# mLSTM with routed experts on one core: k of a pair's heads in one transfer, scores in 64x64 quadrants, the last columns of x and the logits half a step later

## The chip, the cores and the metric

The kernel runs on one core of one Trainium2 chip. The metric is the device time of one execution in microseconds (us). Most executions of a kernel agree within 0.3%.

## What is computed

The reference is an mLSTM layer (a linear attention with gates) followed by a mixture of experts of which each token uses one.

```python
# q, k, v, o_gate: (4, 8, 768, 40) = batch, heads, tokens, dims; i_gate, f_gate: (4, 8, 768)
for t in range(768):
    m_new = maximum(f_gate[t] + m, i_gate[t])
    f, i = exp(f_gate[t] + m - m_new), exp(i_gate[t] - m_new);  m = m_new
    C = f * C + i * outer(v[t], k[t])            # 40 x 40 for each batch and head
    n = f * n + i * k[t]
    y[t] = sigmoid(o_gate[t]) * (C @ q[t]) / maximum(abs(n @ q[t]), 1)
x = y as (4 * 768, 8 * 40)
logits = normalized(x) @ normalized(expert_emb).T / tau      # 8 experts
e = argmax(logits);  out = softmax(logits)[e] * relu(x @ w1[e]) @ w2[e]
```

All inputs are float32. The weights are 320x1024 and 1024x320 for each expert.

## The kernel before

**Tiling.** The recurrence is not run token by token. A window is 128 tokens of one batch entry, and one *half step* n (0 to 23) handles all eight heads of one window: `j, b = divmod(n, 4)` names the window j and the batch entry b. Two half steps, 2q and 2q + 1, share one set of loaded inputs, number q. Within a half step the window is cut into two chunks c of L = 64 tokens. Products inside a chunk are computed directly (a 64x64 matrix of *scores* for each head and chunk, masked by `late` and applied to the gated values `uv`); what comes from earlier tokens goes through a state, `c_st` from one window to the next and `c_mid` from the first chunk to the second.

**How k and q lie.** Heads are held two and two: dims 0 to 39 of one head in partitions 0 to 39, those of the other in partitions 64 to 103. `q_s` holds both, with zeros in the other 48 partitions, and comes in one transfer of 128 partitions. k is held in two tiles: `k_e` has only the upper heads (partitions 0 to 39), `k_o` only the lower ones (64 to 103), and the rest of both is set to zero once per buffer, by memsets and by a multiplication with zero on ScalarE (`zero_act`). `stage_k` issues one transfer of 40 partitions for each. `stage_scores` (line 629) multiplies all 128 rows of `k_e` or `k_o` with all 128 of `q_s`, so that the zeros leave one head. One such product has 64 columns of output partitions (r * 64 onward) and 64 moving columns, and all 16 of a half step go to one bank of PSUM, `s`. `stage_weigh` (line 645) multiplies the bank by the mask on VectorE.

**One half step on TensorE**, in the order of the code: `stage_add(n, 0)` (state and first chunk into the bank `y`, lines 664 and 674), `stage_scores(n + 1)` (line 637), `stage_y(n)` (line 712: weighted scores times `uv`; line 725: q times the two states), `stage_add(n, 1)` (second chunk into the state, line 674). In n = 4 and in the odd n from 5 on, between lines 712 and 725, `stage_xts` transposes what two half steps left of x: 128 tokens, in five pieces of 64 columns for each of two half steps, four pieces to the bank `px` and the fifth to the bank `pj` (line 792). At the end of the same half step `stage_logits` (line 812) multiplies the transposed `xt` by the expert embeddings into the bank `pm`.

**The other engines.** ScalarE copies the state's middle (`c_mid`, line 690), gathers x for the transpose (`xc`, line 785), takes the sum of squares (`junk`, line 771), copies `px` and `pj` to `xt` (lines 798 and 799), takes the sigmoid of the output gate (line 736) and casts pieces of the first expert's weights (line 197). VectorE weighs, normalizes (`den`, `x`) and carries the routing along: `route` appends routing operations to a list, and `tick` takes the next ones off it at fixed places. GpSimd computes `uv`, the output gate's product and parts of the weights. SyncE (SP) issues nearly all transfers.

**What sets the order.** The kernel schedules by hand: each engine runs its instructions strictly in the order in which the code emits them, and waits are placed only where data or a buffer require them. PSUM has eight banks: `pX` one, `pM` two, `pY` three, `pS` one, `pJ` one.

**After the half steps** the last tokens are routed, and the experts run as matrix products of 128 to 512 tokens (lines 390 and 428).

Of the kernel before, what the change touches and what calls it, by code (L numbers as in the profile page):

```python
# [26 lines left out]
P = 128  # L27
# [39 lines left out]
def tile_mlstm_moe(  # L67
# [470 lines left out]
    with ExitStack() as actx:  # L538
# [7 lines left out]
        pS = ictx.enter_context(tc.tile_pool(name="pS", bufs=1, space=PSUM, side="right"))  # L546
        pJ = ictx.enter_context(tc.tile_pool(name="pJ", bufs=1, space=PSUM, side="right"))
# [25 lines left out]
        k_e, k_o, q_s, kv_s, kr_s, vr_s, uv, w_s = [], [], [], [], [], [], [], []  # L573
        for i in range(NB):
            k_e.append(ap1.tile([P, 2, NP, P], F32, name=f"k_e{i}"))
            k_o.append(ap1.tile([P, 2, NP, P], F32, name=f"k_o{i}"))
# [5 lines left out]
            w_s.append(ap1.tile([P, 2, NP, L], F32, name=f"w_s{i}"))  # L582
# [46 lines left out]
        def stage_scores(n):  # L629
            q, k = divmod(n, 2)  # L630
            s = st.setdefault(n, {})["s"] = pS.tile([P, 2, NP, L], F32, name=f"s_{n}", tag="ps")
            for c in range(2):
                cs = slice(c * L, c * L + L)
                for a in range(NP):
                    for r in range(2):
                        m = a // 2 * 2 + r
                        T.matmul(  # L637
                            s[r * L : r * L + L, c, a],
                            (k_e, k_o)[a % 2][q % NB][:, k, m, cs],
                            q_s[q % NB][:, k, m, cs],  # L640
                            start=True,
                            stop=True,
                        )

        def stage_weigh(n):
            V.tensor_tensor(  # L646
                w_s[n % NB].rearrange("p c a t -> p (c a) t"),
                st[n]["s"].rearrange("p c a t -> p (c a) t"),
                late.unsqueeze(1).broadcast_to([P, 2 * NP, L]),
# [55 lines left out]
        def stage_y(n, mid=None):  # L705
# [4 lines left out]
            for a in range(NP):  # L710
                for c in range(2):
                    T.matmul(  # L712
                        y[c * L : c * L + L, a * 2 * D1 : (a + 1) * 2 * D1],
                        w_s[n % NB][:, c, a],
# [72 lines left out]
        def stage_xts(q, pool, tag):  # L787
            xc = xc_.pop(q)
            px = pX.tile([P, 512], F32, name=f"px_{q}", tag="px")
            pj = pool.tile([P, 512], F32, name=f"pj_{q}", tag=tag)  # L790
            for c in range(NX):
                T.transpose(  # L792
                    px[:, c * P : (c + 1) * P] if c < 4 else pj[:, 0:P],
                    xc[:, c].rearrange("p i f -> p (i f)"),
                    ident,
                )
            xt = st[2 * q]["xt"] = tp.tile([P, NX, P], F32, name=f"xt_{q}", tag="xt", bufs=1)
            A.copy(xt[:, 0:4], px.rearrange("p (c t) -> p c t", c=4))
            A.copy(xt[:, 4], pj[:, 0:P])
# [220 lines left out]
        def early_ids():  # L1020
# [18 lines left out]
            5: ([], [(route_a, 0, 0, SAMPLE), (sample,)]),  # L1039
# [7 lines left out]
            15: ([lambda: route_ids(0)], [(route_d, 0), (route_a, 1)]),  # L1047
# [4 lines left out]
        }  # L1052
        vq = []
# [11 lines left out]
        def route(n, i):  # L1065
            if i == 0:
# [15 lines left out]
        def flat(t):  # L1082
            return t.rearrange("p n a t -> p (n a t)")

        def zero_act(t):

            A.activation(
                flat(t).rearrange("p (g t) -> p g t", t=P),
                onef.unsqueeze(1).broadcast_to([P, 2 * NP, P]),
                AF.Copy,  # L1090
                scale=0.0,
            )

        fill(FILLS[0])
        V.memset(k_e[0][:, 0], 0.0)
        G.memset(k_o[0][:, 0], 0.0)
# [6 lines left out]
        V.memset(k_e[0][:, 1], 0.0)  # L1103
# [5 lines left out]
        G.memset(k_o[0][:, 1], 0.0)  # L1109
        G.memset(uv[1], 0.0)  # L1110
        G.memset(c_mid[1], 0.0)
        zero_act(k_e[1])
# [19 lines left out]
        zero_act(k_o[1])  # L1132
# [128 lines left out]
        def embeddings(k):  # L1261
# [3 lines left out]
            elif k == 1:  # L1265
# [5 lines left out]
                zrow = flat(k_e[2])[P - 1 : P]  # L1271
# [18 lines left out]
        for n in range(NS):  # L1290
# [62 lines left out]
            if n == 0:  # L1353
                gates_ends()
                for t in (k_e[2], k_o[2]):
                    zero_act(t)
# [18 lines left out]
            if n == 4 or n >= 5 and n % 2:  # L1375
                turn = lambda: stage_xts((n - 3) // 2, pJ, "pj")
# [13 lines left out]
            if last:  # L1390
                stage_logits((n - 3) // 2)
# [3 lines left out]
                x_tile(xa[0], xs_a[:, 0], 0, pS, "ps")  # L1395
# [90 lines left out]
        stage_xts(n // 2, pM, "pm")  # L1486
# [319 lines left out]
def _layout(q, k, v, i_gate, f_gate, o_gate, moe_expert_emb, moe_tau, moe_w1, moe_w2):  # L1806
# [24 lines left out]
    def by_token(a):  # L1831
# [9 lines left out]
        kt=dims_first(k),  # L1841
# [28 lines left out]
```

## Time and profile before

| | |
|---|---|
| time, median of 3 runs | 325.38 us (324.56 to 326.09) |
| the profiled execution's own time | 328.47 us |
| its span, first to last instruction | 326.7 us |
| TensorE matmul busy, share of the span | 307.4 us, 94% |
| VectorE busy | 217.2 us, 66% |
| ScalarE busy | 164.1 us, 50% |
| GpSimd busy | 146.4 us, 45% |
| moved by DMA | 58.52 MB |
| the half steps | from the start to about 110 us |

The profile names the engines PE (matmuls), PEld (TensorE's weight loads), DVE (VectorE), ACT (ScalarE), POOL (GpSimd) and SP (SyncE). L637 is line 637 of the kernel. A row of a timeline gives the start and the length in us, the engine, the line, the operation, output<-inputs, the shapes and the count; in brackets stands how long the engine had been idle and what ended that. The chain of waits is the work that ended last, followed back from the end; its rows give start, length, engine, tile and line. A float32 matmul of the program is two matmuls in the trace. Durations of matmuls overlap: their ends are modelled, and a busy PE is not a PE at its peak.

### The profile page before, as it was taken

The page shows a single profiled execution, that of the slowest core. Times are in us where ns is not written, and L with a number is a line of the kernel's source. Part 1 is how long each engine was busy: PE and PEld are TensorE (multiplying, and loading weights), DVE is VectorE, ACT ScalarE, POOL GpSimd, SP SyncE. Part 2 cuts the span into 40 slices and gives each one's busy share as a digit, 9 for nine tenths or more (in the row PEclk, how much of TensorE's full clock was granted, in tenths as well). Part 3 has the DMA queues.
Part 4 walks back from the last instruction along what each step waited for, and adds up shares of the span by engine and source line. Part 5 has one row for each costly group of instructions (what it writes and reads, how often), then busy time and mean ns, then how long its engine had stood idle before and what let it go on. Part 6 is the DMA issues. An engine that isn't in the chain of part 4 may idle for free.

```text
span 326.7 us, 9770 instructions
## 1 busy us (share of the span) xinstructions
PE 307.4 (94%) x3769; PEld 290.8 (89%) x3769; DVE 217.2 (66%) x631; ACT 164.1 (50%) x431; POOL 146.4 (45%) x182
## 2 busy tenths in 40 slices
PE   8998999989988879999999999999999999999991
PEld 3787999978876779999999999999999999999990
DVE  5776797897775549796567684574585584766520
ACT  4656556655663695344265463263373463555300
POOL 6659777688784297040635302321251321512121
PEclk9999999999999979999999999999999999999998
DMA  7998797998997523030594964446446465411001
GB/s 228 283 342 252 264 306 238 290 321 272 340 340 219 183 55 113 2 80 3 180 328 168 316 187 134 129 131 191 124 105 247 112 198 198 129 48 42 10 26 33
DMA packets 25101, 58.52 MB, mean 179 GB/s; under 512 B 3707, under 2 KB 10056, under 8 KB 25046
## 3 DMA queue, kind: packets, MB, share of 16 engines
q1 hardware_dynamic: 22166, 48.91, 47.0%
q0 software_dynamic: 2624, 8.48, 8.4%
q8 instruction: 31, 0.51, 0.7%
q10 hardware_dynamic: 256, 0.43, 0.4%
q14 instruction: 24, 0.20, 0.2%
HBM read 49.98 MB, written 8.19 MB: 178 GB/s over the span
## 4 chain that ended last, share of the span: by engine, by line
PE 84%; DVE 4%; DMA 4%; ACT 4%; issue 2%; POOL 1%; POOLq 0%; DVEq 0%; ACTq 0%
PE ph L390 29%; PE po L428 17%; PE s L637 4%; PE po_b L428 4%; PE po_a L428 4%; PE y L712 4%; PE y L674 3%; PE y L725 3%; PE po L415 3%; PE pt L351 2%; PE warm L1078 2%; DMA k_o<-in_kt 2%; PE pm L812 2%; PE px L792 2%; DMA raw<-in_w 2%
## 5 line engine op out<-in xcount | busy, mean ns | idle before, releaser
L447 POOL DMA_INDIRECT out<-ob,ids x20 | 20.3, 1015 | 99.2 <-DVE ob L444 73.7
L622 POOL TENSOR_TENSOR uv<-kv_s,u_t 64x328 f32<-64x328 f32 x47 | 35.3, 751 | 12.7 <-PE y L674 5.4
L428 PE MATMUL po<-w2h,hh 128*128 128x320 f32 x128 | 40.3, 315 | 0.0
L392 ACT ACTIVATE hh<-ph 128x448 fp32r<-128x448 f32 (+2 forms) x48 | 23.7, 493 | 32.7 <-PE ph L390 29.8
L428 PE MATMUL po<-w2h,hl 128*128 128x320 f32 x128 | 39.6, 309 | 0.0
L428 PE MATMUL po<-w2l,hh 128*128 128x320 f32 x128 | 39.5, 309 | 0.0
L394 DVE SCALAR_TENSOR_TENSOR hl<-ph,hh 128x384 fp32r<-128x384 f32 (+1 forms) x48 | 24.5, 511 | 14.6 <-ACT hh L392 12.3
L390 PE MATMUL ph<-xh,w1l 128*128 128x448 f32 (+2 forms) x96 | 32.0, 337 | 0.0
L390 PE MATMUL ph<-xh,w1h 128*128 128x448 f32 (+2 forms) x96 | 32.0, 336 | 0.0
L197 ACT CAST w1h<-raw 128x512 fp32r<-128x512 f32 x48 | 28.9, 616 | 5.4 <-DMA raw<-in_w 4.9
L444 DVE TENSOR_SCALAR ob<-po,gts 128x320 f32<-128x320 f32 x16 | 8.8, 551 | 27.8 <-PE po L428 27.8
L200 DVE TENSOR_TENSOR w2l<-raw,w2h 128x320 fp32r<-128x320 f32 x58 | 26.7, 497 | 0.2
L197 ACT CAST w2h<-raw 128x320 fp32r<-128x320 f32 x64 | 26.1, 461 | 0.0
L637 PE MATMUL s<-q_s,k_e 128*64 128x64 f32 x384 | 24.5, 223 | 1.2 <-DVE w_s L646 1.2
L690 ACT COPY c_mid<-y 40x164 f32<-40x164 f32 x48 | 14.0, 293 | 22.0 <-PE y L674 21.6
L637 PE MATMUL s<-q_s,k_o 128*64 128x64 f32 x384 | 24.5, 222 | 0.5 <-issue 0.5
L390 PE MATMUL ph<-xl,w1h 128*128 128x448 f32 (+2 forms) x96 | 24.6, 337 | 0.0
L312 POOL DMA_INDIRECT xs<-x_d,ids x20 | 21.4, 1070 | 6.9 <-issue 5.5
L200 DVE TENSOR_TENSOR w1l<-raw,w1h 128x512 fp32r<-128x512 f32 x36 | 24.4, 687 | 0.0
L428 PEld LDWEIGHTS po<-w2l,hh 128*128 128x128 f32 x128 | 24.1, 188 | 0.0
L428 PEld LDWEIGHTS po<-w2h,hh 128*128 128x128 f32 x128 | 24.1, 188 | 0.0
L428 PEld LDWEIGHTS po<-w2h,hl 128*128 128x128 f32 x128 | 24.0, 188 | 0.0
(327 smaller groups left out, 922.2 us busy)
## 6 DMA issues: line engine op xcount, KB each, us to landing
raw<-in_w SPq DMA_DIRECT2D x21, 512.0 KB
raw<-in_w SPq DMA_DIRECT2D x32, 320.0 KB
kv_s<-in_rows SPq DMA_DIRECT2D x23, 324.0 KB
q_s<-in_qt SPq DMA_DIRECT2D x11, 512.0 KB
sig<-in_og SPq DMA_DIRECT2D x24, 160.0 KB
x_d<-x SPq DMA_DIRECT2D x24, 160.0 KB
k_e<-in_kt SPq DMA_DIRECT2D x11, 160.0 KB
k_o<-in_kt SPq DMA_DIRECT2D x11, 160.0 KB
```

Of the source, the lines that this page charges most:

```text
L197: A.copy(h, src)
L200: (eng or V).tensor_tensor(lo, src, h.bitcast(F32), ALU.subtract)
L312: G.indirect_dma_start(out=xs[0 : c.shape[0], a, 0:DM], out_offset=None, in_=x_d[0:rows], in_offset=bass.IndirectOffsetOnAxis(ap=c, axis=0 ...
L390: T.matmul(ph, lt, rh, start=i == 0, stop=i == len(ops) - 1)
L392: A.activation(hh, ph, AF.Relu)
L394: V.scalar_tensor_tensor(hl[:, 0:full], ph[:, 0:full], 0.0, hh[:, 0:full].bitcast(F32), ALU.max, ALU.subtract)
L428: T.matmul(po[0 : ts_.stop - ts_.start, 0:DM], lt[f][:, ts_], rh[:, f], start=k == 0, stop=k == len(ops) - 1)
L447: store = G.indirect_dma_start(out=out, out_offset=bass.IndirectOffsetOnAxis(ap=slots, axis=0), in_=ob, in_offset=None, bounds_check=NT - ...
L622: (eng[r] if eng else G).tensor_tensor(uv[n % NB][rows, :, :, r], vr_s[q % NB][rows, k], u_t[rows, j, b].unsqueeze(3).broadcast_to([L, 2, ...
L637: T.matmul(s[r * L : r * L + L, c, a], (k_e, k_o)[a % 2][q % NB][:, k, m, cs], q_s[q % NB][:, k, m, cs], start=True, stop=True,)
L690: A.copy(dst, src)
L712: T.matmul(y[c * L : c * L + L, a * 2 * D1 : (a + 1) * 2 * D1], w_s[n % NB][:, c, a], uv[n % NB][:, c, a].rearrange("p r d -> p (r d)"), s ...
```

## The change

**k.** `k_e` and `k_o` become one tile, `k_s`, laid out as `q_s`: both heads, with the zeros in the other partitions supplied by the host's layout (`both_heads`). `stage_k` issues one transfer of 128 partitions, 512 KB for a pair of half steps, in the place of two of 40 partitions, 160 KB each. The memsets and `zero_act` of k go away. The row of zeros written to `x_d` comes from `c_mid[0]`.

**Scores.** Each product takes 40 rows of one head (from partition 0 or 64) and 64 columns, so it occupies one 64x64 quadrant of the array. Products of upper and lower heads go to two banks: `s` is now two banks, each half used, and `w_s` and `stage_weigh` follow that layout. The bank of `pJ` is given up for it.

**x's fifth piece and the logits.** `stage_xts` is called twice: the four pieces at the old place, and the fifth (`rest=True`) in the next half step, ahead of that half step's scores, into the same bank `px`. `stage_logits` follows those scores. So both now stand in n = 5 and in the even n from 6 on. Two routing steps (`MIDS`) are appended to the list right after the logits, in n = 6 and n = 16, instead of at the end of n = 5 and n = 15. In the last half step the fifth piece and the last tiles of x use a new pool `pT` of two banks.

```diff
-            for r, kk in ((0, k_e), (1, k_o)):
-                SY.dma_start(
-                    kk[q % NB][r * L : r * L + D, ks].rearrange("d n a t -> d (n a t)"),
-                    kt[q, r][:, ks].rearrange("d n a t -> d (n a t)"),
-                )
+            SY.dma_start(
+                k_s[q % NB][:, ks].rearrange("d n a t -> d (n a t)"), kt[q][:, ks].rearrange("d n a t -> d (n a t)")
+            )
...
-            s = st.setdefault(n, {})["s"] = pS.tile([P, 2, NP, L], F32, name=f"s_{n}", tag="ps")
+            s = st.setdefault(n, {})["s"] = pS.tile([P, 2, 512], F32, name=f"s_{n}", tag="ps")
+            sv = s[:, :, 0 : NP * L].rearrange("p h (c i t) -> p h c i t", c=2, i=NP // 2)
             for c in range(2):
                 cs = slice(c * L, c * L + L)
-                for a in range(NP):
-                    for r in range(2):
-                        m = a // 2 * 2 + r
-                        T.matmul(
-                            s[r * L : r * L + L, c, a],
-                            (k_e, k_o)[a % 2][q % NB][:, k, m, cs],
-                            q_s[q % NB][:, k, m, cs],
-                            start=True,
-                            stop=True,
-                        )
+                for i in range(NP // 2):
+                    for h in range(2):
+                        rows = slice(h * L, h * L + D)
+                        for r in range(2):
+                            m = i * 2 + r
+                            T.matmul(
+                                sv[r * L : r * L + L, h, c, i],
+                                k_s[q % NB][rows, k, m, cs],
+                                q_s[q % NB][rows, k, m, cs],
+                                start=True,
+                                stop=True,
+                            )
...
-        def stage_xts(q, pool, tag):
-            xc = xc_.pop(q)
-            px = pX.tile([P, 512], F32, name=f"px_{q}", tag="px")
-            pj = pool.tile([P, 512], F32, name=f"pj_{q}", tag=tag)
-            for c in range(NX):
-                T.transpose(
-                    px[:, c * P : (c + 1) * P] if c < 4 else pj[:, 0:P],
-                    xc[:, c].rearrange("p i f -> p (i f)"),
-                    ident,
-                )
-            xt = st[2 * q]["xt"] = tp.tile([P, NX, P], F32, name=f"xt_{q}", tag="xt", bufs=1)
-            A.copy(xt[:, 0:4], px.rearrange("p (c t) -> p c t", c=4))
-            A.copy(xt[:, 4], pj[:, 0:P])
+        def stage_xts(q, pool=None, tag=None, rest=False):
+
+            xc = xc_[q]
+            if rest:
+                px = pool.tile([P, 512], F32, name=f"pj_{q}", tag=tag)
+            else:
+                px = pX.tile([P, 512], F32, name=f"px_{q}", tag="px")
+                st[2 * q]["xt"] = tp.tile([P, NX, P], F32, name=f"xt_{q}", tag="xt", bufs=1)
+            xt = st[2 * q]["xt"]
+            part = range(4, NX) if rest else range(4)
+            for i, c in enumerate(part):
+                T.transpose(px[:, i * P : (i + 1) * P], xc[:, c].rearrange("p i f -> p (i f)"), ident)
+            A.copy(xt[:, part.start : part.stop], px[:, 0 : len(part) * P].rearrange("p (c t) -> p c t", t=P))
...
+        MIDS = {6: [(route_a, 0, 0, SAMPLE), (sample,)], 16: [(route_a, 1)]}
...
-        V.memset(k_e[0][:, 0], 0.0)
-        G.memset(k_o[0][:, 0], 0.0)
...
+            turned = n > 4 and (n == 5 or n % 2 == 0)
+            if turned:
+                stage_xts((n - 4) // 2, pX, "px", True)
             if not last:
                 stage_scores(n + 1)
+            if turned:
+                stage_logits((n - 4) // 2)
+            route(n, 2)
...
             if n == 4 or n >= 5 and n % 2:
-                turn = lambda: stage_xts((n - 3) // 2, pJ, "pj")
+                turn = lambda: stage_xts((n - 3) // 2)
...
-            if n == 4:
-                stage_logits(0)
-            if n >= 5 and n % 2 and not last:
-                stage_logits((n - 3) // 2)
```

TensorE's instructions from the end of half step 9 into half step 10, before the change (`y_1043` is the bank of half step 9, `y_1164` that of 10, `s_1177` the scores of 11):

```order
L674 MATMUL y_1043<-uv_148,kv_s_153 40x82 x4
L812 MATMUL pm_1124<-ent_138,xt_1107 64x16 x10
L664 MATMUL y_1164<-c_st_164,j_169 40x164 x2
L674 MATMUL y_1164<-uv_154,kv_s_159 40x82 x4
L637 MATMUL s_1177<-q_s_158,k_e_156 64x64 x2
L637 MATMUL s_1177<-q_s_158,k_o_157 64x64 x2
```

After the change, the same place (`y_1021` is half step 9, `y_1127` half step 10, `s_1143` the scores of 11; lines from 630 on have other numbers):

```order
L674 MATMUL y_1021<-uv_144,kv_s_148 40x82 x4
L664 MATMUL y_1127<-c_st_158,j_163 40x164 x2
L674 MATMUL y_1127<-uv_149,kv_s_153 40x82 x4
L798 MATMUL pj_1140<-ident,xc_942 128x128
L637 MATMUL s_1143<-q_s_152,k_s_151 64x64 x16
L814 MATMUL pm_1160<-ent_135,xt_1079 64x16 x10
L712 MATMUL y_1127<-uv_149,w_s_150 64x82 x8
```

The ten products of the logits moved from the end of half step 9 to behind the scores in half step 10, and the fifth transpose moved from half step 9 to ahead of them.

ScalarE's instructions for half steps 9 and 10, before the change (`xc_977` holds half steps 6 and 7, `xc_1173` 8 and 9):

```order
L690 COPY c_mid_167<-y_1043 40x4x41 x2
L785 COPY xc_977<-x_737 128x5x64
L771 ACTIVATE junk_1053,ss_all<-x_737 128x320
L798 COPY xt_1107<-px_1100 128x512
L799 COPY xt_1107<-pj_1101 128x128
L736 ACTIVATE sig_869<-sig_869 128x320
L690 COPY c_mid_166<-y_1164 40x4x41 x2
L785 COPY xc_1173<-x_1081 128x5x64
L771 ACTIVATE junk_1175,ss_all<-x_1081 128x320
```

After the change, from the same `c_mid` of half step 9 on:

```order
L690 COPY c_mid_161<-y_1021 40x4x41 x2
L785 COPY xc_942<-x_717 128x5x64
L771 ACTIVATE junk_1031,ss_all<-x_717 128x320
L799 COPY xt_1079<-px_1078 128x512
L736 ACTIVATE sig_848<-sig_848 128x320
L690 COPY c_mid_160<-y_1127 40x4x41 x2
L785 COPY xc_1136<-x_1059 128x5x64
L771 ACTIVATE junk_1138,ss_all<-x_1059 128x320
L799 COPY xt_1079<-pj_1140 128x128
L736 ACTIVATE sig_848<-sig_848 128x320
```

The copy of the fifth piece moved from half step 9, right behind the copy of the other four, to half step 10, behind that half step's `c_mid`, `xc` and `junk`.

More of the change, by code (lines that the diff above doesn't have):

```diff
@@ L545, in tile_mlstm_moe @@
         ap = ictx.enter_context(tc.tile_pool(name="ap", bufs=2, side="right"))
-        pS = ictx.enter_context(tc.tile_pool(name="pS", bufs=1, space=PSUM, side="right"))
-        pJ = ictx.enter_context(tc.tile_pool(name="pJ", bufs=1, space=PSUM, side="right"))
+        sctx = ExitStack()
+        pS = sctx.enter_context(tc.tile_pool(name="pS", bufs=1, space=PSUM, side="right"))
         rs = ss_all
@@ L571, in tile_mlstm_moe @@
         stage_gates(0)
-        k_e, k_o, q_s, kv_s, kr_s, vr_s, uv, w_s = [], [], [], [], [], [], [], []
+        k_s, q_s, kv_s, kr_s, vr_s, uv, w_s = [], [], [], [], [], [], []
         for i in range(NB):
-            k_e.append(ap1.tile([P, 2, NP, P], F32, name=f"k_e{i}"))
-            k_o.append(ap1.tile([P, 2, NP, P], F32, name=f"k_o{i}"))
+            k_s.append(ap1.tile([P, 2, NP, P], F32, name=f"k_s{i}"))
             q_s.append(ap1.tile([P, 2, NP, P], F32, name=f"q_s{i}"))
@@ L581, in tile_mlstm_moe @@
             uv.append(ap1.tile([P, 2, NP, 2, D1], F32, name=f"uv{i}"))
-            w_s.append(ap1.tile([P, 2, NP, L], F32, name=f"w_s{i}"))
+            w_s.append(ap1.tile([P, 2, 2, NP // 2, L], F32, name=f"w_s{i}"))
         c_st = [ap1.tile([P, NP, 2 * D1], F32, name=f"c_st{b}") for b in range(B)]
@@ L713, in stage_y @@
                         y[c * L : c * L + L, a * 2 * D1 : (a + 1) * 2 * D1],
-                        w_s[n % NB][:, c, a],
+                        w_s[n % NB][:, a % 2, c, a // 2],
                         uv[n % NB][:, c, a].rearrange("p r d -> p (r d)"),
@@ L1065, in route @@
         def route(n, i):
-            if i == 0:
+            if i == 2:
+                vq.extend(f(*a) for f, *a in MIDS.get(n, []))
+            elif i == 0:
                 while vq:
@@ L1108, in tile_mlstm_moe @@
         G.memset(c_mid[0], 0.0)
-        G.memset(k_o[0][:, 1], 0.0)
         G.memset(uv[1], 0.0)
         G.memset(c_mid[1], 0.0)
-        zero_act(k_e[1])
         stage_k(0, slice(1, 2))
@@ L1270, in embeddings @@
                 V.tensor_scalar(en, en, ens, taub[:E], ALU.mult, ALU.mult)
-                zrow = flat(k_e[2])[P - 1 : P]
+                zrow = c_mid[0].rearrange("p m d -> p (m d)")[P - 1 : P]
                 SY.dma_start(x_d[PAD : PAD + 1], zrow[:, 0:DM])
@@ L1354, in tile_mlstm_moe @@
                 gates_ends()
-                for t in (k_e[2], k_o[2]):
-                    zero_act(t)
                 stage_k(2)
@@ L1375, in tile_mlstm_moe @@
             if n == 4 or n >= 5 and n % 2:
-                turn = lambda: stage_xts((n - 3) // 2, pJ, "pj")
+                turn = lambda: stage_xts((n - 3) // 2)
+            if last:
+                sctx.close()
+                pT = ictx.enter_context(tc.tile_pool(name="pT", bufs=2, space=PSUM, side="right"))
             stage_y(n, turn)
@@ L1394, in tile_mlstm_moe @@
                 stage_x(n, late=True)
-                x_tile(xa[0], xs_a[:, 0], 0, pS, "ps")
+                x_tile(xa[0], xs_a[:, 0], 0, pT, "pt")
                 x_tile(xa[0], xs_a[:, 0], 1, pM, "pm")
@@ L1485, in tile_mlstm_moe @@
         work(1, 0)
-        stage_xts(n // 2, pM, "pm")
+        stage_xts(n // 2)
+        stage_xts(n // 2, pM, "pm", True)
         do(1)
```

25 lines of the change are left out of this document (8 added, 17 removed).

## The prediction

> **What bounds the kernel now.** I read the busy shares by stretch first, then the chain of waits inside one stretch, then the timelines of the engines that the chain touches. From 28 us to the end of the half steps, TensorE is the engine that is nearly always busy:
>
> ```profile
> 28.00:58.00 30.00, 29.50 (x757) 27.45 (x755) 22.20 (x89) 18.73 (x59) 21.84 (x39) 1.00 0.85 272
> 58.00:107.00 49.00, 43.14 (x1069) 39.24 (x1069) 38.34 (x124) 28.24 (x85) 35.42 (x40) 1.00 0.92 300
> ```
>
> The columns are the stretch and its length, then the busy us of PE, PEld, DVE, ACT and POOL, the clock, the DMA engines' share and GB/s. PE idles 0.5 us of the first stretch and 5.9 us of the second. The chain of waits for half steps 9 (with a transpose) and 10 (without) is PE alone, so each row's length is the price of that work:
>
> ```profile
> 48.25 0.59 PE px L792 x4
> 48.84 0.11 PE pj L792
> 48.95 0.72 PE y L725 x16
> 49.67 0.28 PE y L674 x8
> 49.95 0.54 PE pm L812 x20
> 50.49 0.30 PE y L664 x4
> 50.80 0.28 PE y L674 x8
> 51.08 0.93 PE s L637 x32
> 52.01 0.57 PE y L712 x16
> ```
>
> A half step is thus set by what PE issues, as long as nobody makes it wait. So the change is judged by two questions: what it takes off PE, and for whom PE then has to wait. The timelines of ACT and PE around the scores of half step 10 answer the second:
>
> ```profile
> 49.36 0.27 ACT L799 COPY xt<-pj 128x128 f32<-128x128 f32 x1
> 50.91 0.29 PE L637 MATMUL s<-q_s,k_e 128*64 128x64 f32 x4
> 51.13 0.60 ACT L690 COPY c_mid<-y 40x164 f32<-40x164 f32 x2 [1.13 <-PE y L674]
> 51.75 0.46 ACT L785 COPY xc<-x 128x320 f32<-128x320 f32 x1
> 51.84 0.46 PE L712 MATMUL y<-uv,w_s 128*64 128x82 f32 x8
> 52.11 0.47 ACT L771 ACTIVATE junk<-x 128x320 f32<-128x320 f32 x1
> ```
>
> ACT sat idle 1.13 us until PE's line 674 released `c_mid`. Whatever is queued behind `c_mid` on ACT cannot run ahead of PE. The scores begin at 50.91 and line 712 follows at 51.84, 0.93 later; ACT is through `c_mid`, `xc` and `junk` only at 52.11 + 0.47 = 52.58, 1.67 after the scores' begin, and then takes the sigmoid `sig`. In the odd half step 11 the same two marks are:
>
> ```profile
> 54.25 0.28 PE L637 MATMUL s<-q_s,k_e 128*64 128x64 f32 x4
> 54.46 0.60 ACT L690 COPY c_mid<-y 40x164 f32<-40x164 f32 x2 [1.43 <-PE y L674]
> 55.18 0.31 PE L712 MATMUL y<-uv,w_s 128*64 128x82 f32 x4
> ```
>
> Line 712 writes the bank from which `c_mid` is copied, and waits for that copy. It ends at 55.06; with 0.05 to react (51.08, the chain's end of line 674, to 51.13, the start of `c_mid`) line 712 could start at 55.11. It starts at 55.18. The 0.93 us of scores hide that wait with 0.07 to spare.
>
> **The change, part by part.**
>
> *Scores in quadrants.* No row shows quadrants; rows show halves. Two instructions with different column halves start together:
>
> ```profile
> 60.09 0.23 PE L725 MATMUL y<-c_st,q_s 128*64 128x82 f32 x1
> 60.10 0.23 PE L725 MATMUL y<-c_mid,q_s 128*64 128x82 f32 x1
> ...
> 25.63 0.28 PE L637 MATMUL s<-q_s,k_o 128*64 128x64 f32 x2
> 25.85 0.34 PE L1277 MATMUL pen<-ident,en 8*64 8x8 f32 x6
> ```
>
> 32 instructions in 0.93 us, two at a time, are 0.06 for a pair. If four go at a time, the scores need 0.47. Against that stand changes of the shape in which the array is used. The four transposes took 0.59 where the fifth took 0.11, so entering them cost 0.15; line 725 took 0.72 behind them and line 712, with as many instructions of that size, 0.57: leaving cost 0.15 too. From 128 rows to 8 rows at 25.85 the next pair came 0.16 after the last (25.63 + 0.06), 0.10 more than the pace. So quadrants cost some 0.14 on entering and 0.14 on leaving. The Trainium skill, "TensorEngine Tiling (Array Packing)", Key Properties, says that changing the tiling mode drains TensorE; by that rule the switches are real, as these rows have it, and without it scores would save 0.46 a half step in place of 0.18.
>
> In odd half steps line 712 then comes at 0.14 + 0.47 + 0.14 = 0.75 after the scores' place, but `c_mid` lets it start only at 55.11 - 54.25 = 0.86. The gain is **0.07**, not 0.46: the rest is a wait that the scores used to cover. If row halves do not overlap, it is 0.28 + 0.93 = 1.21, a loss of 0.28. I take the gain of 0.07, since column halves do overlap.
>
> *Fifth transpose and logits, even half steps.* The copy of the fifth piece now stands on ACT where `sig` stood: it starts at 52.58, takes 0.27 (line 799 above) and ends at 52.85. The last two of the ten logits products need it, the first eight don't. PE gets there early: transpose 0.26, scores 0.75, eight products 0.43, together 1.44 after 50.91, against 1.94 for the copy. So PE waits; 0.05 to react and 4 instructions of the 20 in 0.54 (0.11) put line 712 at 53.01 instead of 51.84: **+1.17** in each of the nine even half steps from 6 to 22. Behind PE's wait is queued everything it does: line 712, line 725, the state, and by that VectorE and GpSimd. Even without any overlap of quadrants PE arrives at 1.90, still before the copy, so this term does not hang on the quadrants. In n = 5 nothing but `c_mid` is ahead of the copy, and PE's own 1.44 counts: +0.51. What goes away: ten times the logits (0.54) and the fifth transpose (0.11) in n = 4 and the odd ones. Together 9 x 1.17 + 0.51 - 10 x 0.65 - 9 x 0.07 (odd n from 7) = **+3.9 us**.
>
> *Routing.* In n = 6 and n = 16, VectorE's routing starts from logits that are now late. Half step 16 shows what stands in that chain (its first reduction, `mx`, came before these rows):
>
> ```profile
> 75.59 0.49 DVE L755 TENSOR_TENSOR x<-y,den 128x320 f32<-128x320 f32 x1
> 76.00 0.21 DVE L856 TENSOR_TENSOR lg_all<-pm,mx 128x64 f32<-128x64 f32 x1
> 76.74 0.69 DVE L646 TENSOR_TENSOR w_s<-s,late 128x512 f32<-128x512 f32 x1 [0.53 <-PE s L637]
> 77.35 0.28 DVE L859 SCALAR_TENSOR_TENSOR cand<-lg_all,wrev_p 128x64 f32<-128x64 f32 x1
> 77.66 0.22 DVE L864 TENSOR_REDUCE m<-cand 128x8 f32<-128x64 f32 x1
> 78.04 0.53 DVE L866 TENSOR_TENSOR oh_all<-cand,m 128x64 bf16<-128x64 f32 x1
> ...
> 75.76 0.95 PE s L637 x32
> 78.62 0.19 PE pm L929
> ```
>
> PE came to line 929 at 76.71 + 0.57 + 0.57 + 0.28 = 78.13 and waited 0.5 for `oh_all`. The chain on VectorE, without its idle 0.53, is 2.4 plus `mx` and `den` (some 0.4, taken as a reduction like L864 and a small operation): 2.8 from the logits' end, less the 1.42 that PE has to do meanwhile, is a wait of 1.4, or 0.9 more than now. In n = 6, with no wait before and smaller tiles, about 1.1. Together **+2.0**, between 0.5 (if part is won back in the next half step) and 2.5.
>
> *Start.* Memsets on DVE, POOL and ACT go away, and SP issues one transfer of k instead of two:
>
> ```profile
> L1087 ACT ACTIVATE k_e<-onef x2: 1040/1050/1060, 3.1 to 11.2; 128x1024 f32<-128x1024 f32 x2
> 0.92 4.88 PE warm L1078 x11
> ```
>
> PE is in its warm-up products until 5.80, and the gates' transfers pace VectorE; the zeros lie beside them. I take 0 for them, and -0.07 for each of the first four half steps' scores: **-0.3**; at best -1.
>
> *DMA.* k costs 512 KB a pair for 2 x 160 KB:
>
> ```profile
> k_e<-in_kt SPq DMA_DIRECT2D x11, 160.0 KB
> q_s<-in_qt SPq DMA_DIRECT2D x11, 512.0 KB
> ```
>
> 192 KB at the 300 GB/s of the second stretch are 0.65 us a pair, 7 us in all. The loads of 28 to 58 us have 15% of free DMA time and are issued four half steps ahead; the second stretch, with 8% free, loads about five pairs, 3.3 us against 3.9 us of free time and the longer half steps. I take 0, at most +3.
>
> *End.* In n = 23 the fifth piece's copy goes behind two others, a copy of `xs_a` (line 342) and the last sigmoid:
>
> ```profile
> 109.18 0.48 ACT L736 ACTIVATE sig<-sig 128x320 f32<-128x320 f32 x1
> ```
>
> Some 0.6 us later, mostly beside the eight other products: **+0.2**.
>
> *What idle time takes up.* Of the 5.9 us that PE idles between 58 and 107 us, part is lateness that longer half steps repair:
>
> ```profile
> PE y L712 <- ACT c_mid L690: 2.2, 4, 0.8
> ```
>
> I take **-0.5**, at most -3. **The sum** is 3.9 + 2.0 - 0.3 + 0.2 - 0.5 = +5.3 us. The profiled execution took 328.5, so 333.8 with a profile; it is 1% above the median of the runs, 325.4, from which the forecast is **330.7 us**. Its own range, with the bounds above, is 328.3 to 333.5.
>
> **The rivals.** (1) *PE's own work sets the pace and the copy is never late*: faster. Then a pair of half steps gains 0.92 by two times 0.46 and loses five more shape changes at 0.15: -0.17; ten pairs, the first half steps and the start at best give -3: 322.4. It decides if ACT is through within 1.44 - 0.05 of the scores' begin; against it is 1.94 in the rows. (2) *Row halves do not overlap*: thirteen half steps without a late copy lose 0.28 instead of gaining 0.07: +4 on the forecast, 334.7. For it: no row shows such overlap. The Trainium skill, "TensorE: Matmul & The Clock Gate", Part 1, has a floor of about 25 ns from start to start; by that the scores would be 0.80, halfway to this rival, but the trace disagrees for column halves, whose starts lie 10 ns apart. (3) *Taken up*: from 58 us on, transfers and VectorE set the pace, and the new wait lies in idle time; -3 for the idle time and 0.5 for the routing: 326.7, hardly slower. Against it: PE is busy 88% there. (4) *Transfers*: the extra bytes make the weights of the first expert late, ACT's casts with them, and `c_mid` behind: +3, 333.7.
>
> **How the numbers follow.** Forecast 0.53, (1) 0.10, (2) 0.13, (3) 0.13, (4) 0.11. The range from 326.0 to 336.5 leaves out (1) and about as much again above and below. What a measurement of this kernel can tell from no change is about 0.5%, 1.6 us. Slower by more than that: the forecast, (2), (4) and a small part of (3), 0.80; within: most of (3), 0.10; faster: (1), 0.10.
>
> **What would show it.** In the profile after: scores in 0.47 to 0.5 us a half step with gaps of 0.1 ahead and behind; in even half steps PE idle some 0.5 us inside line 814 until ACT's line 799, the idle time's largest releaser; in odd ones line 712 right behind `c_mid`. The forecast is wrong if even half steps show no wait on line 799, if odd ones get shorter by more than 0.8 us, or if the transfers' latency grows and `uv` waits for `kv_s`.

## The result, and the profile after

The changed kernel takes **330.03 us** (median of 4 runs, 329.42 to 330.59) against 325.12 us (4 runs). The medians lie 4.9 us, 1.5%, apart; the ratio given with each comparison, and each mean clock, is an estimate from the runs without those in a slower state, here 1.011 with a 95% interval of 1.0067 to 1.0152. In a later comparison the same pair measured 333.64 against 327.51 us, ratio 1.0216 (1.0162 to 1.0271). These two intervals do not overlap, so ratios from different comparisons can be set against each other to about 1% only. The forecast was 330.7 us, 1.6% slower. Below, the time of a half step is the time from line 712 of the one before it to its own line 712.

The chain of waits of the changed kernel, for half step 10:

```profile
51.60 0.30 PE y L674 x8
51.91 0.02 issue
51.93 0.27 ACT c_mid L690
52.20 0.03 issue
52.23 0.29 ACT c_mid L690
52.52 0.03 issue
52.55 0.46 ACT xc L785
53.00 0.46 ACT junk L771 x2
53.47 0.02 issue
53.49 0.28 ACT xt L799
53.77 0.04 issue
53.81 0.30 PE pm L814 x4
54.11 0.61 PE y L712 x16
```

Where the chain before was TensorE alone, it now leaves TensorE at 51.91 and comes back at 53.81: `c_mid`, `xc`, `junk`, and only then the fifth piece. The timelines of TensorE at the same place and in half step 11:

```profile
52.08 0.69 PE L637 MATMUL s<-q_s,k_s 40*64 40x64 f32 x32
52.70 0.65 PE L814 MATMUL pm<-ent,xt 128*64 128x16 f32 x16
53.81 0.30 PE L814 MATMUL pm<-ent,xt 128*64 128x16 f32 x4 [0.47 <-ACT xt L799]
...
56.48 0.69 PE L637 MATMUL s<-q_s,k_s 40*64 40x64 f32 x32
57.24 0.79 PE L712 MATMUL y<-uv,w_s 128*64 128x82 f32 x16
```

Eight of the logits' ten products run at once, the last two (x4) 1.11 us after the first. (The bracket counts from the modelled end of the product before; from start to start the hole is 0.67.) In the odd half step line 712 comes 0.76 after the scores' begin, 0.05 after `c_mid`.

TensorE's waits from 28 to 108 us, first in a second profile of the kernel before, whose execution took 325.45 us, then in the changed kernel (329.42 us). The columns are the wait, its total in us, how often, the longest:

```profile
PE y L712 <- ACT c_mid L690: 1.2, 2, 0.7
PE y L712 <- issue: 0.9, 1, 0.9
PE y L725 <- issue: 0.6, 1, 0.6
PE y L674 <- issue: 0.5, 1, 0.5
PE pm L929 <- DVE oh_all L866: 0.3, 1, 0.3
```

```profile
PE pm L814 <- ACT xt L799: 4.9, 9, 0.9
PE pm L931 <- DVE oh_all L868: 1.8, 1, 1.8
PE pm L877 <- DVE ohf L873: 1.1, 1, 1.1
PE y L712 <- issue: 0.3, 1, 0.3
```

The largest releaser is new; of the routing's two waits that in half step 6 is new and that in half step 16 went from 0.3 to 1.8 us; the waits for "issue", in which nothing shown is waited for, have shrunk. The nine waits on line 799 are that of half step 5 and those of eight of the nine even half steps. In the ninth, half step 12, the copy is as late, but a stall of TensorE lies inside the wait:

```profile
61.74 0.68 PE L814 MATMUL pm<-ent,xt 128*64 128x16 f32 x12 [0.32 <-issue]
61.81 0.27 ACT L799 COPY xt<-pj 128x128 f32<-128x128 f32 x1
```

The last two products start at 62.13, behind the copy, and line 712 comes 1.43 us after `c_mid`, as in the even half steps without a stall. The stall cost nothing there.

Between these two profiles line 712 of the last half step moved from 103.42 to 109.31, 5.9 us, while the end moved by 4.0 us. That the part behind the half steps got 1.9 us shorter is not shown to be the change's doing: it took 219.8 and 220.3 us in the two profiles of before, 218.3 and 219.4 in the two of after, and 217.9 to 221.4 in the variants.

### The profile page after: what moved, and what is told of

The parts are those of the page before. It is cut to its first block, busy times and chain, and to the rows that moved or that the text cites. A ratio compares the mean times of both kernels' runs of the same rounds, so it can differ in the third digit from the quotient of the medians.

```text
span 327.6 us, 9745 instructions
## 1 busy us (share of the span) xinstructions
PE 305.3 (93%) x3769; PEld 283.8 (87%) x3769; DVE 217.9 (67%) x629; ACT 161.6 (49%) x427; POOL 145.2 (44%) x180
## 4 chain that ended last, share of the span: by engine, by line
PE 77%; ACT 8%; DMA 4%; DVE 4%; issue 2%; POOL 2%; SPq 0%; POOLq 0%; ACTq 0%; DVEq 0%
PE ph L390 29%; PE po L428 17%; PE po_b L428 4%; PE y L712 4%; PE po_a L428 4%; PE y L725 3%; PE y L674 3%; PE po L415 3%; ACT c_mid L690 2%; PE pt L351 2%; DMA raw<-in_w 2%; ACT xc L785 2%; PE y L664 2%; PE px L798 1%; DMA kv_s<-in_rows 1%
## 5 line engine op out<-in xcount | busy, mean ns | idle before, releaser
L200 DVE TENSOR_TENSOR w2l<-raw,w2h 128x320 fp32r<-128x320 f32 x58 | 26.0, 485 | 0.2
L712 PE MATMUL y<-uv,w_s 128*64 128x82 f32 x384 | 19.7, 244 | 2.7 <-ACT c_mid L690 1.9
L762 POOL TENSOR_TENSOR x<-x,sig 128x320 f32<-128x320 f32 x20 | 17.4, 877 | 9.6 <-DVE x L755 2.4
```

Of the source, the lines that this page charges most:

```text
L200: (eng or V).tensor_tensor(lo, src, h.bitcast(F32), ALU.subtract)
L712: T.matmul(y[c * L : c * L + L, a * 2 * D1 : (a + 1) * 2 * D1], w_s[n % NB][:, a % 2, c, a // 2], uv[n % NB][:, c, a].rearrange("p r d -> ...
L762: (eng or V).tensor_tensor(x, x, sg, ALU.mult)
```

## The experiments

The runs came from several chips, so each is compared with the kernel before on its own chip. The changed kernel itself was measured in only two of these comparisons. In the edited kernels some line numbers are a few higher: L801 is there the copy of line 799, L816 the logits of line 814.

**The kernel before, once more.**

> The kernel before, unchanged, for a second profile. Its first profiled execution took 328.5 us, 3 us more than the median of its runs, and has three stretches in half steps 19 to 21 (at 86.0, 92.1 and 97.4 us; 2.6 us together) in which TensorE waits for nothing that the profile shows. If these stretches belong to that one execution, the second profile lacks them and takes about 325.5 us. If they belong to the kernel, they stand at the same places and the profiled execution takes about 328.5 us again.

325.45 us, span 323.7. The stalls are not gone: four, 3.0 us together, where the first profile has 4.3 us. Neither reading was right. Two of the four stand at the same place of the program as before (line 725 of half step 18, the 1,870th matmul of the trace, and in line 712 the 2,123rd); the other two are new, and others of the first profile are gone. The places belong to the kernel, and which of them cost anything changes with the execution (more on this in the last section). To set the prediction against the median rather than the slow profiled execution was right.

**The copy ahead of `xc` and `junk`.**

```diff
             stage_mid(n)
+            turned = n > 4 and (n == 5 or n % 2 == 0)
+            if turned:
+                stage_xts((n - 4) // 2, pX, "px", True)
             if n > 5:
                 stage_xc(n - 2)
                 stage_sq(n - 2)
...
-            turned = n > 4 and (n == 5 or n % 2 == 0)
-            if turned:
-                stage_xts((n - 4) // 2, pX, "px", True)
```

> The changed kernel, but ScalarE copies the fifth piece right behind c_mid, ahead of xc and junk; TensorE's order is unchanged. Theory (the copy, queued behind xc and junk, is what the even half steps wait for): the idle 0.67 us inside the logits go away in nine even half steps, 6 us, and the routing of half steps 6 and 16 starts 0.7 us earlier; about 323.5 us, faster than the kernel before by 1.5 us. Rival 1 (TensorE's own work, with its extra changes of shape, is what got longer): the wait moves elsewhere, about 329.5 us. Rival 2 (the larger transfers of k are what costs): unchanged, 330 us.

330.73 us against 326.30, ratio 1.0116 (1.006 to 1.0173): the gain did not come. The wait did go, and what came in its place is in the waits from 28 to 108 us of this kernel:

```profile
PE pm L931 <- DVE oh_all L868: 1.8, 1, 1.8
PE pm L877 <- DVE ohf L873: 1.1, 1, 1.1
PE y L674 <- issue: 1.0, 1, 1.0
PE pm L814 <- ACT xt L799: 0.9, 1, 0.9
PE pm L814 <- issue: 0.9, 1, 0.9
PE y L725 <- issue: 0.7, 1, 0.7
```

Undisturbed even half steps went from 5.02 to 4.37 us as expected. Two things took the time back. First, the stalls: 4.3 us in place of 1.1 (start to start, holes over 0.36 us ahead of a product that waits for no semaphore). Each ends 1.2 to 1.5 us after a 16 KB transfer on the DMA queue of kind "instruction" (worked out from the trace):

```
copy_first: stall 62.04 -> 63.18   instruction transfer 60.77 to 61.70   resumes 1.47 after it
            stall 68.14 -> 69.12                        66.79 to 67.76           1.36
            stall 73.65 -> 74.92                        72.63 to 73.59           1.33
            stall 79.93 -> 80.44                        78.24 to 79.22           1.21
            stall 101.37 -> 101.80                      98.83 to 100.40          1.40
```

Second, the clock: its mean was 0.981 against 0.990 for the kernel before on that chip, at most 3 us of TensorE's work. A cleaner pair for this edit stands further below (two_transfers and copy_first_small).

**Scores with the upper heads first.**

```diff
-            for c in range(2):
-                cs = slice(c * L, c * L + L)
-                for i in range(NP // 2):
-                    for h in range(2):
-                        rows = slice(h * L, h * L + D)
+            for h in range(2):
+                rows = slice(h * L, h * L + D)
+                for c in range(2):
+                    cs = slice(c * L, c * L + L)
+                    for i in range(NP // 2):
```

> The changed kernel, but the scores are issued with all products of the upper heads (array rows from 0) first and then all of the lower ones (from 64), so that neighbours in the queue share their rows and only column halves can overlap. Theory: the scores take 0.94 us instead of 0.48; in even half steps that is hidden by the wait for the copy (TensorE would reach the ninth product at 1.9 after the scores' place, the copy comes at 2.0), in odd ones line 712 comes 0.3 us later: nine times 0.3 and up to 1.5 us in the first half steps, 333 to 334 us. Rival 1 (even half steps are bound by TensorE's own work): 0.46 us in all of them, 338 us or more. Rival 2 (the hardware pairs the quadrants whatever the order, as column halves ran out of program order at 25 us in the first trace): unchanged, 330 us.

334.6 us against 326.3, ratio 1.0272 (1.0216 to 1.0328): the order matters, as the theory had it. TensorE in half step 11:

```profile
59.43 0.98 PE L637 MATMUL s<-q_s,k_s 40*64 40x64 f32 x32
```

The scores took 0.76 from first to last start, between 0.48 and the 0.94 expected. By the pattern of the starts (the trace does not name the rows of a product) the first of the lower sixteen started when ten of the upper sixteen had, so TensorE looked some six of them ahead. Even half steps stayed at 5.02 although their scores were longer by 0.28: they are bound by the copy, not by TensorE's work. Odd ones grew by 0.14 (2.89 to 3.03). Nine times 0.14 is 1.3 us; what the first half steps and the clock (0.982) add was not separated.

**Routing's products one half step later.**

```diff
-            6: ([count_sample], [(choose,)]),
-            7: ([], [(place_rest,)]),
+            7: ([count_sample], [(choose,), (place_rest,)]),
...
-            16: ([lambda: route_rank(1)], [(route_b, 1)]),
-            17: ([], [(route_sum, 1), (route_os, 1, 0, 3)]),
+            17: ([lambda: route_rank(1)], [(route_b, 1), (route_sum, 1), (route_os, 1, 0, 3)]),
```

> The changed kernel, but TensorE's routing products that wait for VectorE (the count of the sample, the ranks of the second group) stand at the end of half steps 7 and 17 instead of 6 and 16, with the VectorE operations that follow them. Theory: the waits of 1.06 us in half step 6 and of 1.83 us in half step 16 go away, and with the second the stretch of 3.4 us behind it in which the granted clock was 0.50 (1.7 us lost): 326 to 327 us. Rival (the time is won back in the next half steps anyway, and the half clock comes from elsewhere): 329.5 us.

332.08 us, ratio 1.0161 (1.0111 to 1.0211): my theory was wrong here. Half steps 7 and 17 did get shorter (4.24 to 2.89, 5.80 to 2.89), but 10 went from 5.02 to 6.86 and 18 from 5.79 to 6.67. In half step 10 the wait moved to where VectorE was late next:

```profile
PE s L637 <- DVE w_s L646: 1.8, 1, 1.8
```

Routing's operations stand in order ahead of `w_s` there, so its cost is VectorE's chain, not the place of the product that waits for it. Half step 18 is another matter: its wait of 1.65 us is on the copy of the fifth piece, and ScalarE was late because a cast of the expert's weights, ahead of `c_mid` in its order, waited for a transfer:

```profile
90.80 0.62 ACT L197 CAST w1h<-raw 128x512 fp32r<-128x512 f32 x1 [1.70 <-DMA raw<-in_w]
```

**k in two transfers, alone and with the early copy.**

```diff
-            SY.dma_start(
-                k_s[q % NB][:, ks].rearrange("d n a t -> d (n a t)"), kt[q][:, ks].rearrange("d n a t -> d (n a t)")
-            )
+            for r in range(2):
+                SY.dma_start(
+                    k_s[q % NB][r * L : r * L + D, ks].rearrange("d n a t -> d (n a t)"),
+                    kt[q, r][:, ks].rearrange("d n a t -> d (n a t)"),
+                )
```

> The changed kernel, but k of a pair comes in two transfers of 40 partitions, 160 KB each, as before the change; the rows between stay unwritten, since quadrant products do not read them. Theory (the 192 KB a pair cost nothing, the even half steps wait for the copy): 329.5 to 330 us, at most 1 us less. Rival (transfers are what costs, since from 58 us on TensorE's instructions come over the same DMA engines and its stalls without a semaphore end 1.2 to 1.7 us after a transfer of instructions): 327 us or less.

331.57 us against 326.66, ratio 1.0162 (1.0116 to 1.0208): no gain is seen from 2.4 MB less, as far as separate comparisons go. The second kernel adds copy_first's edit to this one:

> The fifth piece's copy ahead of xc and junk as in copy_first, and k in two transfers of 40 partitions. New theory after copy_first (the waits of 0.67 us went away in its trace, but stalls for TensorE's instructions rose from 1.1 to 4.3 us, and a stretch at half clock of 1.7 us fell into it): with 1.9 MB less to move between 0 and 100 us the stalls shrink to some 3 us, 328 to 329 us. Rival 1 (the stalls are from TensorE's own demand, whatever else moves): 330.7 us as copy_first. Rival 2 (the half clock was that execution's chance and explains the difference): 326 us or less.

329.94 us, ratio 1.0093 (1.0059 to 1.0127). The two ran on one chip and differ in the copy's place alone: the medians lie 1.6 us apart, where the waits on the copy shrank by some 5 us from start to start (eight undisturbed even half steps at 0.6). The waits from 28 to 108 us, without and with the early copy:

```profile
PE pm L816 <- ACT xt L801: 5.3, 10, 0.9
```

```profile
PE pm L816 <- ACT xt L801: 2.0, 2, 1.0
PE pm L933 <- DVE oh_all L870: 1.8, 1, 1.8
PE pm L879 <- DVE ohf L875: 1.1, 1, 1.1
```

The routing's two waits, 2.9 us together, stay, and the kernel with the early copy is still 3.3 us slower than the kernel before; that the one explains the other was not tested alone. Of the waits on the copy one is that of half step 5. The other, in the transfers' stretch, is not due to `xc` and `junk`: ScalarE stood before it at a cast of the expert's weights.

```profile
67.45 0.62 ACT L197 CAST w1h<-raw 128x512 fp32r<-128x512 f32 x1 [2.15 <-DMA raw<-in_w]
67.97 0.59 ACT L692 COPY c_mid<-y 40x164 f32<-40x164 f32 x2
68.59 0.27 ACT L801 COPY xt<-pj 128x128 f32<-128x128 f32 x1
```

The mean clock fell from 0.986 to 0.980, at most 1.8 us. So of what the early copy frees, part may go into the clock and part into waits for data; how the rest is lost is not shown.

**Quadrants alone.** The order of before, the fifth piece in the free half of a scores' bank:

```diff
+                def turn():
+                    stage_xts((n - 3) // 2)
+                    if not last:
+                        stage_xts((n - 3) // 2, rest=True, bank=st[n + 1]["s"][:, 0, NP * L :])
...
-            if turned:
-                stage_logits((n - 4) // 2)
...
+            if n == 4:
+                stage_logits(0)
+            if n >= 5 and n % 2 and not last:
+                stage_logits((n - 3) // 2)
```

> Only k and the scores are changed: quadrants into two banks, k in one transfer of 128 partitions; the fifth piece is transposed right behind the other four, into the unused half of a scores' bank, and logits and routing stand where they stood before. Theory: the scores' gain is capped by the copy of c_mid, 0.07 us a half step, 1.5 us in all, and 1 us at the start; 323.5 to 324.5 us, faster than the kernel before by 0.3 to 0.9%. Rival 1 (scores shorter by 0.46 and two changes of shape pay fully, 0.18 us a half step): 321 us. Rival 2 (extra changes of shape eat the gain): 326.5 us or more. Rival 3 (what is gained is given back in stalls for instructions): 326 us.

327.62 us against 326.66, ratio 1.0034 (0.9997 to 1.0071): not faster. The bank was a bad choice; the fifth transpose waits for the weighing of the scores beside it, three times, 3.2 us together. One of them, in half step 13:

```profile
66.66 0.33 PE L798 MATMUL s<-ident,xc 128*128 128x128 f32 x1 [1.15 <-DVE w_s L646]
```

The next kernel avoids that: the fifth piece goes to free columns of the logits' bank (`pj = grp[group(q)]["pm"][:, 200:328]`), and k comes in two transfers.

> Quadrants, k in two transfers of 40 partitions, and everything else where it stood before the change; the fifth piece goes to free columns of the logits' bank, so that it waits for no scores. Theory: without the waits of quads_alone on the weighing (4 us in three places), but with the scores' gain still capped by the copy of c_mid (0.03 us a half step in quads_alone) and 0.7 us at the start: 325 to 326 us, within 0.3% of the kernel before. Rival (the quadrants gain 0.18 us a half step once nothing waits): 322.5 us.

327.56 us against 327.51, ratio 1.0005 (0.9969 to 1.004): no difference. In the quiet stretch half steps 6 to 10 take 4.33, 3.15, 4.32, 2.91, 4.32 where before they took 4.36, 3.20, 4.34, 2.93, 4.34: scores half as long gain 0.02 to 0.05 us, because `c_mid` is right behind them: line 712 now starts 0.05 us after the end of `c_mid`. At the start, line 712 of half step 3 came 1.0 us earlier (21.18 for 22.16), but then the clock of this profile fell. By stretch (the clock is the third number from the end):

```profile
27.50:29.00 1.50, 1.50 (x20) 1.23 (x19) 0.73 (x6) 1.22 (x4) 1.22 (x11) 0.53 1.01 268
29.00:31.00 2.00, 2.00 (x36) 1.92 (x34) 1.22 (x6) 1.51 (x6) 1.04 (x2) 0.50 1.02 340
```

**The changed kernel, once more, beside it.**

> The changed kernel unchanged, for a second profile and as the measure for copy_first and copy_first_small beside the same runs of the kernel before (whose median in the later runs is 326.7 us, 1.5 above the first four). Theory: 1.0 to 1.5% above before, 330 to 331.5 us; the waits of 0.68 us at the ninth product of the logits stand in the even half steps again, and those for the routing (1.3 us in half step 6, 2.0 us in 16); the stretch at half clock stands elsewhere or not at all. Rival (the waits belong to one execution): other waits in the second profile.

333.64 us. The same waits at the same places, 5.6 us in nine on line 799, 1.8 and 1.1 for the routing; the half clock stood at 27 us, not at 83. On this chip the changed kernel and quads_pm differ by 6.1 us. Quadrants are in both, and two_transfers showed no gain from k's transfers, so the moved transpose, logits and routing cost some 6 us here, and the quadrants nothing that these runs can tell. On the chip of two_transfers, quads_alone, with k in one transfer, is faster than it by 4.0 us (327.62 for 331.57), so k's transfer does not explain the difference.

**Both waits covered.** Transposes ahead of the scores in odd half steps, so that they cover `c_mid`; logits behind the scores in even ones, except where routing follows:

```diff
             stage_add(n, 0)
-            stage_mid(n)
             if n > 5:
                 stage_xc(n - 2)
+            stage_mid(n)
+            if n == 4 or n >= 5 and n % 2:
+                stage_xts((n - 3) // 2)
+            if n > 5:
                 stage_sq(n - 2)
...
+            if n > 6 and n % 2 == 0 and n != 16:
+                stage_logits((n - 4) // 2)
```

> Quadrants; k in two transfers of 40 partitions; ScalarE's xc ahead of c_mid; in odd half steps all five transposes ahead of the scores, the fifth into free columns of the logits' bank, so that they cover the copy of c_mid; logits behind the scores of the next even half step, where they cover it again, except in half steps 5 and 15, where routing follows and they stay at the end. Theory by TensorE's rows: a pair costs 3.35 us where the same work cost 3.91 before, -0.56 us a pair, 5 us in all, and 1 us at the start: 319 to 321 us. Rival (from 58 us on the gain goes into stalls for instructions, as in copy_first): 323 to 325 us.

328.85 us against 326.66, ratio 1.006 (1.0025 to 1.0095): slower than before. In four odd half steps TensorE met a new wait, of 1.1 to 1.5 us from start to start: ScalarE's `xc`, ahead of the transposes now, waits for the x that GpSimd writes:

```profile
PE px L803 <- ACT xc L788: 4.5, 4, 1.2
```

The stalls for instructions were 3.0 us, the mean clock 0.981.

**Fewer bytes still.** q in two transfers as well, its zeros written once per buffer:

> As copy_first_small, and q too in two transfers of 40 partitions, its zeros written once per buffer (192 KB less for a pair, 384 KB less than in copy_first). Theory (from 58 us on the transfers set the pace, and what an edit takes off TensorE there goes into stalls for instructions and for the expert's weights): 1 MB less from 58 us on is up to 3 us, 327 to 328 us, against 329.9 us for copy_first_small. Rival (it is the routing's waits and the half clock behind them that hold it, not bytes): 329.5 us or more.

334.75 us, ratio 1.0217 (1.016 to 1.0275): slower, with stalls of 5.7 us and a mean clock of 0.976. The changed kernel on the same chip took 333.64 us.

> As quads_pm, with q in two transfers of 40 partitions too. Theory of the transfers' pace: fewer stalls for instructions from 58 us on (3 us in the second profile of the kernel before), 322 to 324 us, faster than before by about 1%. Rival (bytes do not matter): as quads_pm, 325 to 326 us.

329.0 us, ratio 1.0044 (1.0007 to 1.0081), 1.4 us slower than quads_pm beside it. TensorE waited four times for `c_mid`, 5.8 us together. Ahead of `c_mid`, in ScalarE's order, stood in three of the four an operation that waited for a transfer: casts of the weights (1.15 and 2.01 us) and, in the longest, the sigmoid for the output gate:

```profile
26.02 1.02 ACT L741 ACTIVATE sig<-sig 128x320 f32<-128x320 f32 x2 [2.63 <-DMA sig<-in_og]
```

Why these transfers came late is open. The clock was 0.981. Fewer bytes helped in none of the three tries. No version tried beats the kernel before.

## Why the prediction was right, step by step

The mechanism was the one forecast: the late copy in the even half steps and the late routing in two of them. That the sum came out within 1 us is partly luck. The half steps and the routing cost more than forecast, a stretch at half clock came on top, and idle time took up more; these errors have opposite signs. The table sets the steps against the profiles of 325.45 us (before) and 329.42 us (after).

| step | predicted | measured |
|---|---|---|
| scores, odd half step | -0.07 | -0.066 (0.76 + 0.10 for 0.93) |
| even half step, longer before line 712 | +1.17 | +1.31 |
| a pair, undisturbed | +0.45 | +0.64 (7.91 for 7.27) |
| half step 5, with what half step 4 saves (0.51 - 0.65) | -0.14 | +0.42 |
| routing of half steps 6 and 16 | +2.0 | +1.0 and +1.5 |
| start, up to line 712 of half step 3 | -0.3 | -1.0 (second profile after: +0.3) |
| half clock in half steps 17 and 18 | none | about +1.3 |
| k's bytes | 0 | no gain seen from fewer (two_transfers) |
| end | +0.2 | -1.9, not shown to be the change's |
| taken up by idle time | -0.5 | about -3, a remainder |

The half clock is the difference of half steps 17 and 18 between the two profiles of after (5.80 and 5.79 for 5.24 and 5.03). The remainder is what the 5.9 us up to the last line 712 leave when nine pairs, half step 5, routing, start and half clock are taken off.

*Quadrants.* Four at a time, 0.476 from first to last start; entering took 0.10 more than the pace and leaving 0.09. The gain was held to 0.07 by `c_mid` as the prediction had it; quads_pm shows no gain from quadrants alone.

*Even half steps.* The mechanism was the one named. The size was short by 0.14: the copy started 1.56 us after `c_mid` did, not 1.45, since it started only behind the reading out of the sum of squares (the chain's "junk x2"), for which `sig`, in that place before, had not waited (it started 0.1 us ahead of its end); the two late products took 0.14, not 0.11. A pair costs 0.64 rather than 0.45 for that reason and because line 712 itself ran 0.03 to 0.05 slower than in the rows of before.

*Half step 5.* Here the prediction was wrong. It had nothing but `c_mid` ahead of the copy, and its 1.44 of TensorE's work left out the last two products, 0.11. After the change ScalarE first gathered `xc` twice, and could begin only when the fifth transpose had ended, then came `junk`, and then `c_mid`:

```profile
29.53 0.82 ACT L785 COPY xc<-x 128x320 f32<-128x320 f32 x2 [0.43 <-PE pj L798]
```

Line 712 came 2.61 us after the fifth transpose's start; before the change it came 0.93 us after the scores' begin. Against these 1.7 us stand the 0.65 of the logits and the fifth transpose, as forecast, and a wait of 0.66 us ahead of the logits of half step 4 that went away.

*Routing.* VectorE's chain took 3.2 us from the logits' end to `oh_all`, 2.8 were expected. TensorE's wait went from 0.3 to 1.8:

```profile
79.10 0.23 DVE L855 TENSOR_REDUCE mx<-pm 128x8 f32<-128x64 f32 x1 [2.94 <-PE pm L814]
80.60 0.47 DVE L861 SCALAR_TENSOR_TENSOR cand<-lg_all,wrev_p 128x64 f32<-128x64 f32 x1
81.48 0.81 DVE L868 TENSOR_TENSOR oh_all<-cand,m 128x64 bf16<-128x64 f32 x1
```

`cand` and `oh_all` took 0.47 and 0.81 where the first profile had 0.28 and 0.53.

*Taken up.* This is the term that was mis-sized most: -0.5, with -3 as its bound. Stalls of TensorE without a semaphore were 3.0 and 4.3 us in the two profiles of before and 1.1 in both of after; waits on `c_mid` went from 1.2 to 0.2 us. In kernels that keep the wait for the copy the stalls were 0.4 to 1.1 us (five profiles), in those without it mostly 3 to 5.7 (0 and 1.2 in two). In half step 12 the rows show a stall that lies inside the new wait; that the others vanished for the same reason is argued, not shown.

*Rivals.* (1) is out: the copy was late in every even half step. (2) is out: row halves overlap. (4) is not seen as far as k's bytes go; that a late transfer holds up a cast or a sigmoid on ScalarE, and `c_mid` behind it, does occur in three of the variants (copy_first_small, route_later, quads_pm_kq). (3) was partly right: the time is not hidden, but about a third of it is.

## What to carry to other kernels

Before work is moved ahead of a point where an engine must be reached early, list what stands on the other engine's queue ahead of the operation that it will wait for: here 1.6 us of `c_mid`, `xc` and `junk` against 1.2 us of TensorE's work. An operation that hides a wait is worth only what it exceeds the wait by: scores half as long gained 0.03 us. And where an engine is stalled by several things in turn, the length of one wait is not what its removal brings: some 5 us of waits, 1.6 us of time.

## What the hardware showed that was not expected

**Half clock after a short idle.** In the first profile of the changed kernel TensorE waited 1.83 us for `oh_all`; 0.7 us after it resumed, the granted clock was 0.50 for 3.4 us:

```profile
81.00:82.25 1.25, 0.00 (x0) 0.00 (x0) 1.22 (x4) 0.00 (x0) 1.25 (x2) 1.00 1.02 391
82.25:83.00 0.75, 0.66 (x15) 0.57 (x16) 0.69 (x5) 0.00 (x0) 0.67 (x2) 1.00 0.95 345
83.00:84.00 1.00, 1.00 (x24) 0.78 (x22) 0.91 (x6) 0.26 (x1) 0.72 (x1) 0.52 0.93 315
84.00:85.00 1.00, 1.00 (x34) 0.88 (x30) 0.22 (x2) 0.96 (x4) 0.86 (x1) 0.50 1.00 368
85.00:86.00 1.00, 1.00 (x17) 0.82 (x13) 0.96 (x4) 0.28 (x2) 0.00 (x0) 0.50 0.99 353
```

The Trainium skill, "TensorE: Matmul & The Clock Gate", Part 1, has the clock halved after an idle window of some 3.4 us: the length of the slow stretch agrees, but no idle stretch as long stood ahead of it here. The same wait of 1.8 us in two_transfers and copy_first was not followed by one. In all fourteen profiles every change of the clock lies a whole number of 3.41 us after the first one of that execution (here 83.03 - 4.53 = 23 times 3.41). In the 3.41 us ahead of this drop TensorE was busy for 1.58 us; in the same place of that grid in copy_first, 81.57 to 84.98 us, it was busy for 1.58 us too, and the clock stayed. So a half-idle stretch is enough at times, not always, and what decides is open.

Such a stretch stood between 26 and 39 us in nine of the twelve profiles with quadrants and in neither of before, which are only two. The mean clock over the runs was 0.988 to 0.991 for the kernel before and 0.976 to 0.990 for the others, a difference of at most 5 us of TensorE's work. That shorter scores lower TensorE's load enough to cause it is argued, not shown.

**Stalls at fixed places of the program.** Between 28 and 108 us the fourteen profiles have 39 holes of over 0.36 us ahead of a product that waits for no semaphore. All but two end 1.1 to 1.8 us after a 16 KB transfer of kind "instruction", which come every 3 to 8 us; the two (2.3 and 2.5 us after) follow another hole closely. Counted in matmuls of the trace, 34 of the 39 stand within six of the 1,108th or a multiple of 127 behind it (the 1,235th, 1,362nd and so on to the 2,251st). In before_again exactly 256 instructions of TensorE, weight loads included, lie between the first two of them, the 1,360th and the 1,487th, and the 16 KB transfers also come once for some 255 instructions. So these are the places where TensorE needs its next block of instructions, and there it waits for them. At most of these places it does not wait; what makes a block late is open, since fewer bytes of k and q did not end it.
